# Block-selected attention with a gated MLP: who copies the selection rows, who normalises, and how the last outputs leave

## The chip, the cores and the metric

The kernel runs on one core of a Trainium2 chip. The metric is the device time of one execution in microseconds (us), the median of several runs. Engines are named as in the profile: PE is TensorE (matmuls; PEld are its weight loads), DVE is VectorE, ACT is ScalarE, POOL is GpSimd, and SP is the engine that issues the DMA transfers.

## What is computed

Attention over 4 batches of 8 heads, 768 positions, 64 values per head. For each query the keys are seen in 24 chunks of 32; an upper bound of the query's product with each chunk is made from the chunk's minimum and maximum, and only the 6 best chunks, causally masked, take part. The result is the input of a gated MLP block.

```python
# attention, per head; chunk = 32, top_k = 6
ub = sum(maximum(q * k_min, q * k_max))           # per query and chunk, causal
sel = the 6 chunks with the largest ub
attn = softmax(where(sel & causal, q @ k.T / 8, -1e9))
x = attn @ v                                      # heads side by side: (4, 768, 512)
# the MLP block
h = gelu_tanh(x @ w_in)                           # 512 -> 1024
u, v = h[..., :512], h[..., 512:]
v_n = (v - mean(v)) / sqrt(var(v) + 1e-6) * g_ln
v_s = w_sg @ v_n + b_sg[:, None]                  # over the positions, 768 x 768
out = x + (u * v_s) @ w_out
```

## The kernel before

The 32 heads are worked in 16 pairs (p = 0 to 15, two heads i = 0, 1 on 64 partitions each). Pairs 0 to 3 belong to batch 0 and so on; every four pairs, a batch of the MLP block (b = 0 to 3) follows, mixed with the scores of later pairs.

Each operation of the program is recorded once, by a call of `P.op` (or of the helper `flex`, L429 to L442), with an engine, a tag and what it reads and writes. The order of the work is not the order of the text: `TABLE` at the end holds, for each engine, the list of the operations' numbers in the order in which that engine runs them, the PSUM slot of each tile, the number of idle matmuls ahead of an operation (`filler`) and the engine of those operations that may run on several (`engine`). `place` and `link` turn this into one in-order queue for each engine and into semaphore waits. So an operation that waits holds everything behind it on its engine. SP's queue holds all transfers, loads, transposing transfers and stores alike. On POOL an operation marked `shift` also waits for its neighbour.

The tags that the text uses, with the pair or batch behind them:

- ktr, qtr (L524): K and Q of a pair transposed on PE, three 128-column matmuls each; kev, qev (L435, L438): the copies of these from PSUM to KA, qT; kmm (L563): minimum and maximum of each chunk on DVE, four instructions for a pair; wsub: their difference; rel (L435, L437): relu of qT; qcast, vcast, kcast (L435, L438): casts to bf16 into QA, vx, kbx.
- kT (L587), dt_x (L882): transposing transfers on SP, of K for pairs 12 to 15 and of the attention output (xT) for batches 1 and 2.
- ub (L662, L709): the bounds on PE; utr, m8, dn, dt (L718, L729, L734, L737): transposed on DVE, the sixth largest found by max8, compared, and transposed back into Dt. For the pairs from 4 on, `select_full` works two pairs at a time. qd (L742): the rows of Dt, 32 partitions by 576 for each head, are put into QA[w][i], where 32 spare rows carry the mask into the score matmul. Before, qd is a transfer on SP.
- sc (L778, L818): scores, in pieces of 1024 columns; exp (L784, L833): their exponential on ACT; aff (L789, L840): the causal mask of the diagonal blocks on POOL; pv, pvd (L856, L863): the product with V, pvd for the masked diagonal; rcp, xs (L871, L873): the division into XS.
- hv, gv, bns, bna (L905, L909, L914, L916): the v half, its gelu and statistics per 128 positions; var, rstd, nmr (L918, L920, L922): the reciprocal deviation, raised to the power on POOL; vhat (L928 on ACT, L933 on DVE): the normalised v, six tiles of 128 x 512 per batch.
- hu, gu (L945, L950): the u half; pt (L962): w_sg times vhat, which needs all six vhat of its batch; vs, gt (L968, L972): scale, bias and gate on DVE; ou (L981): the last product; os (L988): the residual sum into one of three buffers osb; st (L992): the store, 128 x 512 fp32.

PSUM is used in two halves: two slots of 1024 columns for scores, and four of 512 for the rest.

Of the kernel before, what the change touches and what calls it, by code (L numbers as in the profile page):

```python
# [261 lines left out]
def _build(nc, ctx, q, k, v, w_in, g_ln, w_sg, b_sg, w_out, out):
    B, H, S, DH = q.shape
    DM = H * DH
# [428 lines left out]
    def select_full(pairs, u, v_):  # L693
# [45 lines left out]
        for x, p in enumerate(pairs):  # L739
            for i in range(2):  # L740
                w, g0 = p % NW, 32 * (2 * (1 - i) + x)
                P.op("sp", lambda e, w=w, i=i, g0=g0: e.dma_start(  # L742
                    QA[w][i][g0:g0 + 32, LO:S], Dt[v_][g0:g0 + 32].rearrange("p a b -> p (a b)")), dmac(590),
                    ("qd", p, i), reads=[("Dt", v_)], writes=[("QD", w, i)], dma=f"qd{w}_{i}", xfer=150)
# [133 lines left out]
    def xtrans(b, dk):  # L878
        src = XS[:, b % 2, dk]
        rd = [("XS", b % 2, 2 * dk), ("XS", b % 2, 2 * dk + 1)]  # L880
        if (b, dk) in DXT:
            P.op("sp", lambda e: e.dma_start_transpose(xT[b % 2][:, dk, :].rearrange("p (t x) -> p t x", x=128),  # L882
# [13 lines left out]
    def moe_h(b):  # L896
# [28 lines left out]
        for qt in range(NT):  # L925
# [6 lines left out]
            else:  # L932
                o = P.op("dve", lambda d, qt=qt: d.tensor_scalar(vhat[s][:, qt, :], vg[qt], mv[s][:, qt, 0:1],  # L933
                                                                 rstd[s][:, qt:qt + 1], op0=ALU.subtract,
                                                                 op1=ALU.mult),
                         (456, 548), ("vhat", b, qt), port=True,
                         reads=[("vg", qt), ("mv", s, qt), ("nmr", s), ("rstd", s)], writes=[("vhat", s, qt)])
# [16 lines left out]
    def moe_g(b):  # L954
        s = b % 2
        for tg in range(2):
# [19 lines left out]
            for qt in range(3 * tg, 3 * tg + 3):  # L976
                t = ps_g.tile((2, 3) if b < B - 1 else None)

                def ou(e, t=t, qt=qt):
# [7 lines left out]
                os_ = (b * NT + qt) % 3  # L987
                P.op("dve", lambda d, t=t, qt=qt, os_=os_: d.tensor_tensor(  # L988
                    osb[os_][:].rearrange("p (a x) -> p a x", x=128),
                    t.ap()[:, 0:DM].rearrange("p (a x) -> p a x", x=128), XS[:, b % 2, :, qt, :], op=ALU.add), dve(DM), ("os", b, qt),  # L990
                    reads=[t] + [("XS", b % 2, hh) for hh in range(H)], writes=[("osb", os_)], ps=[t])
                P.op("sp", lambda e, qt=qt, os_=os_: e.dma_start(  # L992
                    bass.AP(out.tensor, (b * S + 128 * qt) * DM, [[DM, 128], [1, DM]]), osb[os_][:]), dmac(),
                    ("st", b, qt), reads=[("osb", os_)], dma=f"o{os_}", xfer=680)
# [208 lines left out]
```

## Time and profile before

| | us |
|---|---|
| median of 3 runs (lowest, highest) | 219.81 (219.38, 221.41) |
| the profiled execution | 220.97 |
| its span, first to last instruction | 219.1 |
| PE busy | 205.8 |
| DVE busy | 185.9 |
| ACT busy | 169.5 |
| POOL busy | 93.2 |

The mean granted clock of TensorE is 0.982 of full. How to read the rows: a row of a timeline has the start, the length (several instructions of one kind merged), the engine, the line, the operation, what it writes and reads, and in brackets the idle time before it and what ended it. A row of a group has the line, the count, the busy time and the mean of one in ns. A row of waits has who waited for whom: the sum in us, the number of times and the longest. A row of the chain has start, length, engine and line. "SPq" rows are issues of transfers. Ends of matmuls are modelled, so a PE that is busy is not always at its peak.

### The profile page before, as it was taken

The page shows a single profiled execution, that of the slowest core. Times are in us where ns is not written, and L with a number is a line of the kernel's source. Part 1 is how long each engine was busy: PE and PEld are TensorE (multiplying, and loading weights), DVE is VectorE, ACT ScalarE, POOL GpSimd, SP SyncE. Part 2 cuts the span into 40 slices and gives each one's busy share as a digit, 9 for nine tenths or more (in the row PEclk, how much of TensorE's full clock was granted, in tenths as well). Part 3 has the DMA queues.
Part 4 walks back from the last instruction along what each step waited for, and adds up shares of the span by engine and source line. Part 5 has one row for each costly group of instructions (what it writes and reads, how often), then busy time and mean ns, then how long its engine had stood idle before and what let it go on. Part 6 is the DMA issues. An engine that isn't in the chain of part 4 may idle for free.

```text
span 219.1 us, 5967 instructions
## 1 busy us (share of the span) xinstructions
PE 205.8 (94%) x2357; PEld 134.1 (61%) x2357; DVE 185.9 (85%) x536; ACT 169.5 (77%) x256; POOL 93.2 (43%) x130
## 2 busy tenths in 40 slices
PE   7799999999999999997998989998799999999991
PEld 3477777846767577783355666776545669545640
DVE  3889999799999999998799987985896876968982
ACT  3778999979899899998668888998768978575000
POOL 8434699894374556464023537185102414002000
PEclk9879999999999999998899999999999999999999
DMA  7999999993999988947999849642955004000325
GB/s 153 249 219 205 223 211 375 294 237 124 248 225 238 208 231 200 225 81 135 263 233 179 141 81 224 75 113 56 217 105 124 0 0 146 3 0 0 144 87 201
DMA packets 95067, 35.48 MB, mean 162 GB/s; under 512 B 89280, under 2 KB 90048, under 8 KB 95040
## 3 DMA queue, kind: packets, MB, share of 16 engines
q1 hardware_dynamic: 95040, 35.11, 72.6%
q8 instruction: 18, 0.29, 0.6%
q14 instruction: 9, 0.07, 0.1%
HBM read 24.77 MB, written 6.29 MB: 142 GB/s over the span
## 4 chain that ended last, share of the span: by engine, by line
PE 63%; DVE 16%; ACT 11%; DMA 4%; issue 3%; SPq 0%; DVEq 0%
PE PSG L962 11%; PE PSG L945 7%; PE PSG L905 7%; PE PSC L778 7%; PE PSG L524 6%; ACT E L784 5%; PE PSG L856 4%; PE PSG L981 4%; DMA QA<-Dt 4%; DVE osb L988 3%; PE PSG L709 3%; PE PSC L818 3%; PE PSG L662 3%; DVE Wall L563 2%; DVE U L718 2%
## 5 line engine op out<-in xcount | busy, mean ns | idle before, releaser
L784 ACT ACTIVATE E<-PSC 128x1024 bf16<-128x1024 f32 (+1 forms) x72 | 63.4, 916 | 8.2 <-PE PSC L778 7.0
L778 PE MATMUL PSC<-QA,KA 128*128 128x128 bf16 (+2 forms) x336 | 37.2, 246 | 2.2 <-ACT E L784 1.2
L962 PE MATMUL PSG<-wsgT,vhat 128*128 128x384 bf16 x192 | 35.3, 326 | 0.6 <-DVE vhat L933 0.6
L789 POOL TENSOR_SCALAR_AFFINE_SELECT E<-E 128x768 bf16<-128x768 bf16 x24 | 21.1, 885 | 30.6 <-ACT E L784 30.2
L778 PEld LDWEIGHTS PSC<-QA,KA 128*128 128x128 bf16 x336 | 24.3, 98 | 12.6 <-ACT E L784 3.2
L438 POOL CAST QA<-qT 64x768 bf16<-64x768 f32 (+1 forms) x24 | 20.6, 860 | 22.1 <-ACT qT L435 13.4
L905 PE MATMUL PSG<-winb,xT 128*128 128x512 bf16 x96 | 24.4, 397 | 1.8 <-DVE XS L873 1.1
L962 PEld LDWEIGHTS PSG<-wsgT,vhat 128*128 128x128 bf16 x192 | 17.8, 98 | 11.8 <-ACT qT L435 1.0
L563 DVE TENSOR_REDUCE Wall<-PSG 128x12 f32<-128x384 f32 x48 | 24.7, 540 | 0.3 <-PE PSG L524 0.2
L945 PE MATMUL PSG<-xT,winb 128*128 128x384 bf16 x128 | 24.4, 327 | 0.0
L950 ACT ACTIVATE uT<-PSG 128x384 bf16<-128x384 f32 x32 | 15.5, 490 | 11.3 <-PE PSG L945 10.6
L981 PE MATMUL PSG<-woutb,uT 128*128 128x512 bf16 x96 | 23.7, 379 | 0.0
L909 ACT ACTIVATE vgb<-PSG 128x512 f32<-128x512 f32 x24 | 14.3, 598 | 11.0 <-PE PSG L905 10.9
L968 DVE SCALAR_TENSOR_TENSOR PSG<-PSG,glnT,bsgbc 128x384 f32<-128x384 f32 x32 | 19.5, 618 | 2.4 <-PE PSG L962 2.3
L920 POOL TENSOR_TENSOR rstd<-rstd,neghalf 128x6 f32<-128x6 f32 x4 | 5.3, 1330 | 37.5 <-DVE rstd L918 37.5
L833 ACT ACTIVATE E<-PSC 128x1024 bf16<-128x1024 f32 (+1 forms) x24 | 20.7, 918 | 0.2
L856 PE MATMUL PSG<-vx,E 128*128 128x65 bf16 x480 | 19.9, 194 | 0.4 <-DVE osb L988 0.3
L988 DVE TENSOR_TENSOR osb<-PSG,XS 128x512 f32<-128x512 f32 x24 | 16.0, 683 | 5.0 <-PE PSG L981 4.0
L914 DVE BATCH_NORM_STATS2 stats<-vgb 128x6 f32<-128x512 f32 x24 | 16.2, 681 | 3.2 <-ACT vgb L909 3.0
L856 PEld LDWEIGHTS PSG<-vx,E 128*128 128x128 bf16 x480 | 17.3, 98 | 2.3 <-DVE osb L988 0.6
L873 DVE TENSOR_TENSOR XS<-PSG,rden 128x384 bf16<-128x384 f32 x32 | 17.6, 554 | 0.6
L972 DVE TENSOR_TENSOR uT<-PSG,uT 128x384 bf16<-128x384 f32 x32 | 17.3, 550 | 0.5
(106 smaller groups left out, 370.8 us busy)
## 6 DMA issues: line engine op xcount, KB each, us to landing
qn<-in_q_dram SPq DMA_DIRECT2D x32, 192.0 KB, 4.5
vn<-in_v_dram SPq DMA_DIRECT2D x16, 384.0 KB, 5.5
out_dram<-osb SPq DMA_DIRECT2D x24, 256.0 KB, 2.7
kn<-in_k_dram SPq DMA_DIRECT2D x24, 192.0 KB, 4.6
uT<-in_moe_w_sg_dram SPq DMA_DIRECT2D x4, 384.0 KB, 5.8
vgb<-in_moe_w_in_dram SPq DMA_DIRECT2D x3, 512.0 KB, 9.1
kn<-in_k_dram SPq DMA_DIRECT2D x4, 384.0 KB, 4.5
QA<-Dt SPq DMA_DIRECT2D x24, 36.0 KB, 2.6
```

The costliest lines, as they stand in the source:

```text
L438: return e.tensor_copy(dst(), src())
L563: P.op("dve", lambda d, m=m, op=op, t=t, hf=hf: d.tensor_reduce(W[w][:, m, 12 * hf:12 * hf + 12], t.ap()[:, 0:TG].rearrange("p (c x) -> p ...
L778: r = e.matmul(t.ap()[:, o:o + n], KA[w][i][:, 128 * kb:128 * kb + 128], QA[w][i][:, q0:q0 + n], start=True, stop=True)
L784: P.op("act", lambda e, t=t, c0=c0, c1=c1, i=i: e.activation(E[es][:, i, c0:c1], t.ap()[:, 0:c1 - c0], ACTF.Exp, scale=SCALE), act(c1 - c0 ...
L789: P.op("pool", lambda g, ev=ev: g.affine_select(ev, ev, pattern=[[0, NT], [1, 128]], compare_op=ALU.is_ge, fill=0.0, base=0, channel_multi ...
L833: P.op("act", lambda e, t=t, c0=c0, c1=c1, n=n: e.activation(E[es][:, :, c0:c1], t.ap().rearrange("p (i x) -> p i x", i=2)[:, :, 0:n], ACT ...
L856: r = e.matmul(t.ap()[:, 65 * qb:65 * qb + 65], E[es][:, i, a:a + 128], vx[w][:, kb, i, :], start=first, stop=False, skip_group_check=True)
L905: r = e.matmul(t.ap()[:, 0:F], xT[s][:, dk, 128 * qt:128 * qt + 128], winb[:, dk, F:DFF], start=(dk == 0), stop=(dk == NDK - 1))
L945: r = e.matmul(t.ap()[:, 0:TG], winb[:, dk, 128 * fb:128 * fb + 128], xT[s][:, dk, TG * tg:TG * tg + TG], start=(dk == 0), stop=(dk == NDK ...
L962: r = e.matmul(t.ap()[:, 0:TG], vhat[s][:, sb, 128 * fb:128 * fb + 128], wsgT[:, sb, TG * tg:TG * tg + TG], start=(sb == 0), stop=(sb == N ...
L981: r = e.matmul(t.ap()[:, 0:DM], gT[s][:, fb, 128 * qt:128 * qt + 128], woutb[:, fb, :], start=(fb == 0), stop=(fb == NF - 1))
L988: P.op("dve", lambda d, t=t, qt=qt, os_=os_: d.tensor_tensor(osb[os_][:].rearrange("p (a x) -> p a x", x=128), t.ap()[:, 0:DM].rearrange(" ...
```

## The change

Four things are edited in the program, and the whole table is written anew.

1. qd becomes a `flex` operation: a copy on POOL, or on DVE or ACT where the table says so. Of the 24, POOL has 14, ACT five (qd_4_1, qd_5_1, qd_9_1, qd_10_0, qd_11_0), DVE five (qd_10_1, qd_11_1, qd_13_0, qd_15_0, qd_15_1).
2. vhat may also run on POOL, as a tensor_scalar with two per-partition scalars. Of the 24, POOL has 14 (0_1, 0_2, 0_4, 0_5; 1_0, 1_1, 1_2, 1_3, 1_5; 2_3; 3_0, 3_2, 3_4, 3_5), ACT four (0_3, 1_4, 3_1, 3_3), DVE six (0_0 and five of batch 2). Before, DVE had 19 and ACT five.
3. For the last three position blocks of the last batch, os and st are made in halves of 256 columns, the sum goes into the buffers qn (free by then) in place of osb, and a store of the last batch may be issued by ACT; four are (st_3_2, st_3_4_0, st_3_5_0, st_3_3_256).
4. The engine of the transposing transfers becomes a name that the table may change. It does not: all stay on SP.

```diff
-                P.op("sp", lambda e, w=w, i=i, g0=g0: e.dma_start(
-                    QA[w][i][g0:g0 + 32, LO:S], Dt[v_][g0:g0 + 32].rearrange("p a b -> p (a b)")), dmac(590),
-                    ("qd", p, i), reads=[("Dt", v_)], writes=[("QD", w, i)], dma=f"qd{w}_{i}", xfer=150)
+                flex("pool", ("dve", "act"), lambda w=w, i=i, g0=g0: QA[w][i][g0:g0 + 32, LO:S],
+                     lambda g0=g0: Dt[v_][g0:g0 + 32].rearrange("p a b -> p (a b)"), NSEL, ("qd", p, i), [("Dt", v_)],
+                     [("QD", w, i)], shift=True)
...
-                o = P.op("dve", lambda d, qt=qt: d.tensor_scalar(vhat[s][:, qt, :], vg[qt], mv[s][:, qt, 0:1],
+                o = P.op(eng, lambda d, qt=qt: d.tensor_scalar(vhat[s][:, qt, :], vg[qt], mv[s][:, qt, 0:1],
...
+                last, os_ = b == B - 1 and qt > 2, (b * NT + qt) % 3
+                dst = qn[os_][:].rearrange("p i t d -> p (i t d)")[:, 0:DM] if last else osb[os_][:]
+                names = [("qn", os_, 0), ("qn", os_, 1)] if last else [("osb", os_)]
+                for c0, c1 in ((0, DM // 2), (DM // 2, DM)) if last else ((0, DM),):
+                    P.op("dve", lambda d, t=t, qt=qt, dst=dst, c0=c0, c1=c1: d.tensor_tensor(
...
+                    o = P.op(ENG.get("_".join(str(x) for x in tag), "sp"), lambda e, qt=qt, dst=dst, c0=c0, c1=c1: e.dma_start(
+                        bass.AP(out.tensor, (b * S + 128 * qt) * DM + c0, [[DM, 128], [1, c1 - c0]]), dst[:, c0:c1]), dmac(),
...
     "filler": (
-        "50:8 "),
+        "49:8 58:2 83:2 "),
```

Number 49 is ktr_0_0, 58 is qtr_0_0 and 83 is ktr_1_0. The new lists, given by tag where the text below speaks of them:

- PE, the start: ktr_0_0 ktr_0_1 qtr_0_0 qtr_0_1 ktr_1_0 ktr_1_1 ub_0 (before: ktr_0_1 ktr_0_0 qtr_0_1 qtr_0_0 ktr_1_1 ub_0 qtr_1_0 qtr_1_1 ktr_1_0). DVE: kmm_0 four times, qev_0_1, wsub_0, kmm_1 four times, then the selection of pair 0 (before: kev_0 twice, kmm_0 four times, rel_0, wsub_0, two of kmm_1, the selection, the other two of kmm_1). kev_0 and rel_0 are on ACT.
- PE, into batch 1: pvd_7_1 pv_7_0 pvd_7_0 ktr_11_1 sc_8_1_0 sc_8_1_1 qtr_12_0 sc_8_1_2 ktr_10_1 ktr_10_0 hv_1_1 sc_8_0_1 sc_9_1_1 hv_1_0 (before: pvd_7_1 ktr_11_1 sc_8_1_2 sc_8_1_0 ktr_10_0 sc_8_1_1 ktr_10_1 hv_1_1 hv_1_0 sc_8_0_0). POOL does qd_8_1 and qd_8_0 behind aff_7_0. kev_11_1 (two instructions) goes from ACT to DVE, qd_9_1 is on ACT.
- PE, the end of hv in batch 1: hu_1_2_0 hv_1_4 hu_1_3_1 ub_10 hu_1_3_0 hu_1_0_1 qtr_13_1 hu_1_0_0 qtr_13_0 hu_1_1_1 qtr_12_1 hu_1_2_1 hu_1_1_0 perm_12 pt_1_0_1. POOL: rstd_1 vhat_1_1 vhat_1_5 vhat_1_0 vhat_1_2 vhat_1_3 aff_8_1. perm_12 is a small permutation by matmul (L602).
- PE, around 131 us before: pt_1_0_3 sc_8_0_2 sc_9_0_1 ub_12 sc_10_1_2 (before: sc_9_0_1 pv_8_1 pvd_8_1 sc_10_1_0). rel_12 and rel_14 go from ACT to DVE.
- PE, in batch 3: the six hv, then hu hu ou_2_3 ou_2_4, six hu, ou_2_5, then pt. POOL: rstd_3 and the four vhat.
- DVE, the end: os_3_2 gt_3_1_2 os_3_1 os_3_0 os_3_4_256 os_3_4_0 os_3_5_0 os_3_5_256 os_3_3_256 os_3_3_0. The last number is the half's first column.

Other casts and evictions change engines too: nine casts and mask rows leave POOL for ACT and seven come back, and evictions are exchanged between DVE and ACT (on balance DVE takes two more of them and three more rel).

More of the change, by code (lines that the diff above doesn't have):

```diff
@@ L494, in _build @@
     QRUN = [0] * 16
+    TENG = "sp"
     KRUN = [0] * 16
@@ L586, in kside_full @@
                  ("kcast", p, i), [("kn", s, 0), ("kn", s, 1), ("kbi", n, i)], [("kbx", n, i)])
-            P.op("sp", lambda e, i=i: e.dma_start_transpose(
+            P.op(ENG.get(f"kT_{p}_{i}", TENG), lambda e, i=i: e.dma_start_transpose(
                 KA[w][i][:].rearrange("p (t x) -> p t x", x=128), kbx[n][:, i].rearrange("p t c -> p (t c)")), dmac(1250),
@@ L881, in xtrans @@
         if (b, dk) in DXT:
-            P.op("sp", lambda e: e.dma_start_transpose(xT[b % 2][:, dk, :].rearrange("p (t x) -> p t x", x=128),
+            P.op(ENG.get(f"dt_x_{b}_{dk}", TENG), lambda e: e.dma_start_transpose(xT[b % 2][:, dk, :].rearrange("p (t x) -> p t x", x=128),
                                                        src.rearrange("p t c -> p (t c)")), dmac(1250), ("dt_x", b, dk),
@@ L932, in moe_h @@
             else:
[L933 to L936, printed above, removed]
+                o = P.op(eng, lambda d, qt=qt: d.tensor_scalar(vhat[s][:, qt, :], vg[qt], mv[s][:, qt, 0:1],
+                                                               rstd[s][:, qt:qt + 1], op0=ALU.subtract,
+                                                               op1=ALU.mult),
+                         (456, 548) if eng == "dve" else (590, 640), ("vhat", b, qt), port=True,
                          reads=[("vg", qt), ("mv", s, qt), ("nmr", s), ("rstd", s)], writes=[("vhat", s, qt)])
-            o.alts = {"act": (704, 809), "dve": (456, 548)}
+            o.alts = {"act": (704, 809), "dve": (456, 548), "pool": (590, 640)}
         for fb in range(NF):
@@ L986, in moe_g @@
                      writes=[t], alloc=t)
[L987 to L994, printed above, removed]
+                last, os_ = b == B - 1 and qt > 2, (b * NT + qt) % 3
[3 more added lines that the diff above has]
+                    P.op("dve", lambda d, t=t, qt=qt, dst=dst, c0=c0, c1=c1: d.tensor_tensor(
+                        dst[:, c0:c1].rearrange("p (a x) -> p a x", x=128),
+                        t.ap()[:, c0:c1].rearrange("p (a x) -> p a x", x=128), XS[:, b % 2, c0 // 128:c1 // 128, qt, :],
+                        op=ALU.add), dve(c1 - c0), ("os", b, qt) + ((c0,) if last else ()),
+                        reads=[t] + [("XS", b % 2, hh) for hh in range(c0 // 64, c1 // 64)],
+                        writes=names if not last else [("qn", os_, c0 // 256)], ps=[t])
+                    tag = ("st", b, qt) + ((c0,) if last else ())
+                    o = P.op(ENG.get("_".join(str(x) for x in tag), "sp"), lambda e, qt=qt, dst=dst, c0=c0, c1=c1: e.dma_start(
+                        bass.AP(out.tensor, (b * S + 128 * qt) * DM + c0, [[DM, 128], [1, c1 - c0]]), dst[:, c0:c1]), dmac(),
+                        tag, reads=names if not last else [("qn", os_, c0 // 256)],
+                        dma=f"o{os_ + 3 * last}_{c0}", xfer=680 if not last else 360)
+                    if b == B - 1:
+                        o.alts = {"sp": (610, 610), "act": (571, 571)}
     SEL, GRP, UB, u = {}, {}, {}, 0
```

19 lines of the change are left out of this document (15 added, 4 removed), and 115 rows, old and new, of the table TABLE.

## The prediction

> **What bounds the kernel now.** I read the page's busy shares, then the table of stretches, then the waits, and last the timeline and the chain where TensorE's clock or busy time falls. In a stretch's row stand its length, the busy time of each engine and, behind the last bracket, TensorE's granted clock.
>
> ```profile
> PE 205.8 (94%) x2357; PEld 134.1 (61%) x2357; DVE 185.9 (85%) x536; ACT 169.5 (77%) x256; POOL 93.2 (43%) x130
> ```
>
> ```profile
> 44.00:98.00 54.00, 53.14 (x605) 37.62 (x603) 51.87 (x163) 49.47 (x83) 31.06 (x42) 1.00 0.92 203
> 98.00:106.00 8.00, 6.05 (x32) 2.58 (x30) 6.21 (x12) 6.50 (x10) 3.07 (x5) 0.79 0.89 163
> ...
> 170.00:211.00 41.00, 41.00 (x361) 25.43 (x361) 33.25 (x69) 23.97 (x33) 7.11 (x8) 1.00 0.11 39
> ```
>
> TensorE is full from 170 to 211 us and nearly so from 44 to 98. It does the same matmuls after the change, so what can move is the start, the hole at 98 to 106, a few gaps between 116 and 157 and the tail. What leaves VectorE elsewhere is worth nothing by itself.
>
> ```profile
> PEld PSC L778 <- ACT E L784: 3.2, 7, 0.8
> ...
> PE PSC L778 <- DMA QA<-Dt: 0.9, 2, 0.6
> ```
>
> TensorE waits 0.9 us in all for the transfers that the change removes; the exponentials on ScalarE (ACT) hold it longer.
>
> **The start.** Four idle matmuls are added, two ahead of qtr_0_0 and two ahead of ktr_1_0, and the first K evictions go from VectorE to ScalarE.
>
> ```profile
> 8.39 0.52 PE L524 MATMUL PSG<-identF,kn 128*128 128x128 f32 x3 [0.97 <-DMA kn<-in_k_dram]
> 9.52 0.93 PE L662 MATMUL PSG<-qT,Wall 64*32 64x288 f32 x8 [0.61 <-DVE Wall L573]
> ```
>
> ```profile
> 10.00:11.00 1.00, 1.00 (x12) 0.38 (x6) 0.87 (x2) 0.09 (x1) 0.00 (x0) 0.50 1.23 276
> ```
>
> ```profile
> 1.25 4.02 PE PSC L359 x9
> ...
> 7.15 1.85 DVE Wall L563 x4
> ...
> 9.52 2.12 PE PSG L662 x18
> 11.63 1.93 PE PSG L524 x9
> ...
> 15.61 1.22 PE PSG L662 x18
> ...
> 49.13 0.66 PE PSG L524 x6
> ...
> 55.75 0.65 PE PSG L945 x4
> ```
>
> After idle times of 0.97 and 0.61 us the clock is 0.50: the 18 matmuls of ub_0 take 2.12 instead of 1.22 us and the next nine 1.93 instead of 0.99, 1.84 lost. An idle matmul takes 4.02/9 = 0.45 us, so two of them cover 0.9 of the 0.97; I take the dip as avoided. But the new VectorE order has all four kmm_1 reductions ahead of the first selection instead of two: two more, at 1.85/4 each, give 0.95 back. Net -0.9, between -1.9 (nothing given back) and +0.5 (the dip stays and the idle matmuls delay qtr_0).
>
> The Trainium skill, "TensorE: Matmul & The Clock Gate", Part 1, says that the clock falls after at least one idle window of about 3.4 us. By that rule gaps of 0.97 and 0.61 us would not have dropped it and the added matmuls would be worth nothing; the row with 0.50 says otherwise, and I go by the row.
>
> **98 to 106 us.** The rows for the scores of pair 8 come late, and the second half clock follows.
>
> ```profile
> 99.45 0.61 PE L778 MATMUL PSC<-QA,KA 128*128 128x384 bf16 x4 [0.50 <-ACT E L784]
> 100.46 0.55 PE L524 MATMUL PSG<-identF,kn 128*128 128x128 f32 x3 [0.39 <-ACT KA L435]
> 101.65 3.30 PE L905 MATMUL PSG<-winb,xT 128*128 128x512 bf16 x8 [0.65 <-DMA xT<-XS]
> 105.28 0.65 PE L778 MATMUL PSC<-QA,KA 128*128 128x128 bf16 x7 [0.34 <-DMA QA<-Dt]
> ```
>
> ```profile
> 96.30 4.20 SPq L882 DMA_TRANSPOSE xT<-XS  x2
> ...
> 101.18 0.71 SPq L742 DMA_DIRECT2D QA<-Dt  x1
> ```
>
> ```profile
> 191.10 1.73 PE PSG L905 x8
> ```
>
> Waits of 0.50 + 0.39 + 0.65 + 0.34 = 1.88, and eight matmuls in 3.30 instead of 1.73: 3.45 in all. The copy of the rows stood on SP behind two transposing transfers, from 96.30 on. On POOL it needs no queue: the 0.34 goes, and two evictions (kev_11_1) leave ScalarE. The transposes stay on SP, and hv_1_1 still needs the last of them, so most of the 0.65 stays. Whether the clock dips again I can't tell: about 1.5 us of idle time caused it at the start, and about as much is left here. I take half of the 1.57: -1.5 in all, between 0 and -3.2.
>
> **Normalisation.** Fourteen vhat go to POOL; VectorE keeps 6 of 19, ScalarE 4 of 5. No row shows a tensor_scalar on POOL; the nearest are casts of the same size and, as an upper end, one that was held up.
>
> ```profile
> L438 POOL CAST woutb<-osb x1: 611/611/611, 66.9 to 66.9; 128x512 bf16<-128x512 f32 x1
> ```
>
> ```profile
> L438 POOL CAST vx<-vn x14: 826/832/1407, 21.2 to 172.5; 128x768 bf16<-128x768 f32 x14
> ```
>
> ```profile
> 109.59 1.04 PE L905 MATMUL PSG<-winb,xT 128*128 128x512 bf16 x4
> ...
> 112.79 1.33 POOL L920 TENSOR_TENSOR rstd<-rstd,neghalf 128x6 f32<-128x6 f32 x1 [11.65 <-DVE rstd L918]
> ...
> 117.84 1.14 PE L962 MATMUL PSG<-wsgT,vhat 128*128 128x384 bf16 x6 [0.60 <-DVE vhat L933]
> ```
>
> I take 0.61, between 0.61 and 1.41. In batch 1 the last group of hv ends at 109.59 + 1.04 = 110.6 and rstd at 112.79 + 1.33 = 114.1; vhat was there by 117.8. With 0.5 for nmr and five vhat on POOL it is 114.6 + 5 x 0.61 = 117.7, the same. TensorE meanwhile has seven hu groups of 0.65, ub_10 (1.2, as ub_0 at full clock), three transposes of 0.33 and the small perm_12, to 117.6: the wait of 0.60 shrinks, -0.2, between -0.6 and, at 1.41 each (121.7), +3.5. In batches 0 and 3 four vhat on POOL (2.4) stand behind the same 4.0 us from the last hv to nmr (114.6 - 110.6), 6.4 in all. To cover them TensorE has seven hu groups, five transposes and two score groups in batch 0, about 6.9, and eight hu and three ou (0.86, as a group of hv) in batch 3, 7.8: nothing; at 1.41 each, 3.2 more, +2.6 and +1.7. Batch 2 moves one.
>
> The Trainium skill, "GPSIMD Engine Reference", 3.1, has 1.8 cycles per element at 1.2 GHz, 768 ns for 512 elements; by that estimate batch 1 would be 0.8 later than I take it and the sum would be 0.8 higher.
>
> **Selection rows.** Of 24 copies (32 partitions by 576 elements), POOL gets 14, ScalarE 5, VectorE 5; SP's queue loses all 24.
>
> ```profile
> L438 POOL COPY KA<-INDF 64x768 bf16<-64x768 bf16 x8 | 6.6, 823 | 0.3
> ...
> L435 ACT ACTIVATE rT<-qT 128x576 f32<-128x576 f32 x11 | 7.5, 683 | 0.1
> ...
> L438 DVE COPY xT<-PSG 128x768 bf16<-128x768 bf16 x5 | 2.8, 553 | 0.6 <-PE PSG L890 0.6
> ```
>
> By these rows 0.62 on POOL (823 x 576/768), 0.68 on ScalarE, 0.41 on VectorE, whose 13 vhat fewer pay for it. They count at the gaps where rows or exponentials were awaited:
>
> ```profile
> 130.71 0.60 PE L778 MATMUL PSC<-QA,KA 128*128 128x128 bf16 x7 [0.70 <-ACT E L784]
> ...
> 149.16 0.60 PE L778 MATMUL PSC<-QA,KA 128*128 128x128 bf16 x7 [0.59 <-DMA QA<-Dt]
> ...
> 156.11 1.02 PE L905 MATMUL PSG<-winb,xT 128*128 128x512 bf16 x4 [1.10 <-DVE XS L873]
> ```
>
> At 149 us the transfer goes: -0.55 (0 to -0.6; next late is the exponential two score tiles back). At 131 rel_12 (0.68) leaves ScalarE and ub_12 stands ahead of the scores: -0.5 (0 to -0.7). At 156 TensorE waits for xT, a transpose that stays on SP with less ahead of it: -0.2 (-0.7 to +0.6).
>
> Against that: POOL's order gets 14 x 0.62 + 14 x 0.61 = 17 us of work, less about 2 for casts that leave it; its masks (aff), which gate pvd, stand behind. Its busy share rises from 43 to about 50%, so it is a matter of single late masks: +0.8 (0 to +2). ScalarE gets eight instructions before 62 us (qcast_4_1, mrow_1_1_0, two row copies, vhat_0_3, three wev) and loses, the exchanged evictions set against each other, three; five more at 0.5 to 0.8, in a stretch where TensorE seldom waits for it: +0.6 (0 to +2).
>
> **The tail.**
>
> ```profile
> 213.69 1.03 PE L981 MATMUL PSG<-woutb,uT 128*128 128x512 bf16 x4
> ```
>
> ```profile
> 213.27 0.69 DVE L988 TENSOR_TENSOR osb<-PSG,XS 128x512 f32<-128x512 f32 x1 [0.41 <-DMA out_dram<-osb]
> 214.46 1.29 DVE L988 TENSOR_TENSOR osb<-PSG,XS 128x512 f32<-128x512 f32 x2 [0.50 <-DMA out_dram<-osb]
> ```
>
> ```profile
> DMA to landing us min/median/max: 2.0/2.1/2.9
> ```
>
> The last three outputs wait 0.41 + 0.50 for their buffer; in qn they don't. The last matmul ends at 213.69 + 1.03 = 214.7; two halves of about 0.40 (estimated, a little over half of 0.69) follow, so VectorE ends at 215.5 instead of 215.75, and the last store is 128 KB on one of two queues (2.0 to 2.9 us, the lower end likelier): -0.6, between -0.2 and -1.1.
>
> **Sum.** -0.9 - 1.5 - 0.2 - 0.55 - 0.5 - 0.2 - 0.6 = -4.45; +0.8 + 0.6 = +1.4; net -3.05. The profiled execution took 220.97 us, 1.87 more than its span of 219.1; it would take 217.9. It stands 1.16 above the median of the three runs, 219.81, which becomes 216.8.
>
> **The rivals.** (a) POOL becomes the bound, slower. If a vhat costs 1.41 there, as the held-up cast did, pt_1 comes 3.5, pt_0 2.6 and pt_3 1.7 us later, in place of the -0.2: 216.8 + 8.0 = 224.8; it decides from about 1.05 us each, where the three delays sum to 3. For it: the row with 1407 against a median of 832, and a vhat of VectorE that ended with a POOL cast beside it after 1049 ns against a median of 541. Against it: those medians. The Trainium skill, "SBUF — State Buffer", section on the two separate sides, says that VectorE and GpSimd share a port pair under an exclusive lock, the loser blocked for the whole instruction; the two maxima agree.
>
> ```profile
> L933 DVE TENSOR_SCALAR vhat<-vgb,mv,rstd x19: 505/541/1049, 57.4 to 200.1; 128x512 bf16<-128x512 f32 x19
> ```
>
> (b) The transfers were hidden anyway and the waits change hands: both clock dips stay (+0.9 and +0.8 against my sum, and the gaps at 131 and 156 stay for ScalarE's and the transposes' sake, +0.7): 216.8 + 2.4 = 219.2. For it: 0.9 us in the row of waits, against 3.2 for the exponentials. (c) Both dips go, nothing is given back and no mask is late: -0.95 - 0.8 - 1.4 more: 213.6.
>
> **How the numbers follow.** Forecast 0.45, (a) 0.17, (b) 0.26, (c) 0.12. A difference of under 1% (2.2 us) is about what can't be told from none; the forecast's own spread (215.0 to 218.3) puts a seventh of it there. Faster: 0.38 + 0.12 + 0.06 of (b) = 0.56; the same: 0.07 + 0.18 + 0.02 of (a) = 0.27; slower: 0.15 + 0.02 = 0.17. The range from (c) to the mild end of (a), 213.4 to 220.6, leaves out some 0.2.
>
> **What would show it.** Clock 1.00 from 9 to 16 us and ub_0 in about 1.2 us show the start right. No wait of TensorE on Dt's rows, and the first hv of batch 1 in 0.43 or 0.22 per matmul, show the hole. POOL's vhat at 0.6 to 0.8 us shows the normalisation; 1 us and more, with pt waiting on POOL, makes me wrong towards (a). No idle time of VectorE behind out_dram, and an end about 3.8 us behind the last matmul instead of 4.4, show the tail. New waits of pvd on POOL's masks or of scores on ScalarE beyond 1.4 us make me wrong towards (b).

## The result, and the profile after

The changed kernel takes 242.65 us (median of 4 runs, 242.51 to 244.37) against 220.36 us (219.38 to 221.41): 1.103 times the time before, with a 95% interval of 1.095 to 1.111. The forecast was 216.8 us, with a range of 213.4 to 220.6. It is wrong in sign. A median here is over all executions of a kernel, while a ratio leaves out those in which the chip was in a slower state, so the two can differ by some tenths of a per cent. Rival (a), POOL as the bound, is what happened, at a price well above the one that the rival was given.

The profiled execution of the change has a span of 242.5 us (before 219.1). The page's busy shares come first, then the waits of TensorE and the price of a vhat (median in the middle of the three figures, in ns).

```profile
PE 209.4 (86%) x2346; PEld 135.8 (56%) x2361; DVE 185.5 (77%) x536; ACT 171.4 (71%) x257; POOL 128.3 (53%) x156
```

```profile
PE PSG L963 <- POOL vhat L934: 18.0, 3, 7.3
```

```profile
L934 POOL TENSOR_SCALAR vhat<-vgb,mv,rstd x14: 2070/2073/2347, 58.2 to 221.0; 128x512 bf16<-128x512 f32 x14
```

VectorE's and ScalarE's busy times hardly change. POOL has 35 us more. TensorE waits three times, 18.0 us in all, for vhat on POOL; a vhat there takes 2.07 us, not 0.61.

To see whether anything else was lost, cut each execution at two events of each batch: the end of nmr, from which vhat can start, and the start of the first vs, which needs pt and so all six vhat. In the kernel before, VectorE's rows are these:

```profile
57.24 0.15 DVE L922 SCALAR_TENSOR_TENSOR nmr<-mv,rstd 128x6 f32<-128x6 f32 x1
61.57 0.62 DVE L968 SCALAR_TENSOR_TENSOR PSG<-PSG,glnT,bsgbc 128x384 f32<-128x384 f32 x1
...
114.36 0.12 DVE L922 SCALAR_TENSOR_TENSOR nmr<-mv,rstd 128x6 f32<-128x6 f32 x1
119.21 0.60 DVE L968 SCALAR_TENSOR_TENSOR PSG<-PSG,glnT,bsgbc 128x384 f32<-128x384 f32 x1
...
166.04 0.17 DVE L922 SCALAR_TENSOR_TENSOR nmr<-mv,rstd 128x6 f32<-128x6 f32 x1 [1.44 <-POOL rstd L920]
170.06 0.63 DVE L968 SCALAR_TENSOR_TENSOR PSG<-PSG,glnT,bsgbc 128x384 f32<-128x384 f32 x1 [0.19 <-PE PSG L962]
...
198.51 0.17 DVE L922 SCALAR_TENSOR_TENSOR nmr<-mv,rstd 128x6 f32<-128x6 f32 x1 [0.41 <-POOL rstd L920]
202.06 0.62 DVE L968 SCALAR_TENSOR_TENSOR PSG<-PSG,glnT,bsgbc 128x384 f32<-128x384 f32 x1 [0.23 <-PE PSG L962]
```

After the change, VectorE's rows and between them POOL's:

```profile
57.95 0.17 DVE L923 SCALAR_TENSOR_TENSOR nmr<-mv,rstd 128x6 f32<-128x6 f32 x1
58.22 8.52 POOL L934 TENSOR_SCALAR vhat<-vgb,mv,rstd 128x512 bf16<-128x512 f32 x4 [0.30 <-DVE nmr L923]
69.00 0.63 DVE L969 SCALAR_TENSOR_TENSOR PSG<-PSG,glnT,bsgbc 128x384 f32<-128x384 f32 x1 [6.73 <-PE PSG L963]
...
121.71 0.17 DVE L923 SCALAR_TENSOR_TENSOR nmr<-mv,rstd 128x6 f32<-128x6 f32 x1
121.98 10.30 POOL L934 TENSOR_SCALAR vhat<-vgb,mv,rstd 128x512 bf16<-128x512 f32 x5 [0.30 <-DVE nmr L923]
134.54 0.63 DVE L969 SCALAR_TENSOR_TENSOR PSG<-PSG,glnT,bsgbc 128x384 f32<-128x384 f32 x1 [8.14 <-PE PSG L963]
...
181.73 0.17 DVE L923 SCALAR_TENSOR_TENSOR nmr<-mv,rstd 128x6 f32<-128x6 f32 x1 [1.46 <-POOL rstd L921]
186.39 0.63 DVE L969 SCALAR_TENSOR_TENSOR PSG<-PSG,glnT,bsgbc 128x384 f32<-128x384 f32 x1 [0.62 <-PE PSG L963]
...
214.52 0.17 DVE L923 SCALAR_TENSOR_TENSOR nmr<-mv,rstd 128x6 f32<-128x6 f32 x1 [0.27 <-POOL rstd L921]
214.79 8.25 POOL L934 TENSOR_SCALAR vhat<-vgb,mv,rstd 128x512 bf16<-128x512 f32 x4 [0.30 <-DVE nmr L923]
225.30 0.63 DVE L969 SCALAR_TENSOR_TENSOR PSG<-PSG,glnT,bsgbc 128x384 f32<-128x384 f32 x1 [6.57 <-PE PSG L963]
```

The stages, as differences of these rows (end of nmr is start plus length; the last stage ends with the span):

| stage | before, us | after, us | difference |
|---|---|---|---|
| start to nmr of batch 0 | 57.4 | 58.1 | +0.7 |
| nmr to first vs, batch 0 | 4.2 | 10.9 | +6.7 |
| first vs of batch 0 to nmr of batch 1 | 52.9 | 52.9 | 0.0 |
| nmr to first vs, batch 1 | 4.7 | 12.7 | +7.9 |
| to nmr of batch 2 | 47.0 | 47.4 | +0.4 |
| nmr to first vs, batch 2 | 3.9 | 4.5 | +0.6 |
| to nmr of batch 3 | 28.6 | 28.3 | -0.3 |
| nmr to first vs, batch 3 | 3.4 | 10.6 | +7.2 |
| to the end | 17.0 | 17.2 | +0.2 |

The four normalisations lose 22.5 of the 23.4 us. The five other stages together lose 0.9 where the forecast had them gain about 2.85. The execution before holds the two half-clock stretches that the prediction read at 10 and 102 us, so an execution of the old kernel without them would make these five look slightly worse.

Behind each long wait TensorE's clock falls as well. In the rows of stretches the granted clock stands behind the last bracket:

```profile
66.00:71.00 5.00, 4.12 (x14) 2.21 (x15) 1.26 (x3) 0.00 (x0) 3.54 (x5) 0.50 0.91 197
...
132.00:136.00 4.00, 3.57 (x13) 2.07 (x14) 1.31 (x4) 0.49 (x1) 2.67 (x4) 0.50 0.22 52
...
223.00:227.00 4.00, 3.82 (x13) 1.83 (x14) 1.18 (x2) 0.00 (x0) 0.04 (x1) 0.50 0.00 0
```

The first pt tile therefore takes 2.08 us where it took 1.14, which adds about 0.9 to each of the three stages.

```profile
132.43 2.08 PE L963 MATMUL PSG<-wsgT,vhat 128*128 128x384 bf16 x6 [7.29 <-POOL vhat L934]
```

The waits before these stretches were 5.5, 7.3 and 5.2 us. The granted clock falls 3.5, 4.5 and 3.8 us into them, stays at half for 6.8 us, and is back at 1.00 only 4.8, 4.1 and 5.5 us after TensorE has gone on. The Trainium skill, "TensorE: Matmul & The Clock Gate", Part 1, has the clock fall after an idle window of about 3.4 us; in these three waits the trace agrees with it.

### The profile page after: what moved, and what is told of

It reads as the page before. It is cut to its first block, busy times and chain, and to the rows that moved or that the text cites. A ratio compares the mean times of both kernels' runs of the same rounds, so it can differ in the third digit from the quotient of the medians.

```text
span 242.5 us, 5963 instructions
## 1 busy us (share of the span) xinstructions
PE 209.4 (86%) x2346; PEld 135.8 (56%) x2361; DVE 185.5 (77%) x536; ACT 171.4 (71%) x257; POOL 128.3 (53%) x156
## 4 chain that ended last, share of the span: by engine, by line
PE 53%; DVE 15%; POOL 14%; ACT 6%; DMA 6%; issue 3%; POOLq 1%; SPq 1%; DVEq 0%
PE PSG L963 15%; POOL vhat L934 10%; PE PSC L779 7%; PE PSG L906 5%; PE PSG L982 5%; PE PSG L857 4%; PE PSG L525 4%; DMA vn<-in_v_dram 3%; DMA kn<-in_k_dram 3%; PE PSG L946 3%; DVE stats L915 2%; ACT E L785 2%; PE PSG L864 2%; DVE Wall L564 2%; POOL rstd L921 2%
## 5 line engine op out<-in xcount | busy, mean ns | idle before, releaser
L963 PE MATMUL PSG<-wsgT,vhat 128*128 128x384 bf16 x192 | 41.1, 367 | 18.0 <-POOL vhat L934 18.0
L963 PEld LDWEIGHTS PSG<-wsgT,vhat 128*128 128x128 bf16 x192 | 19.9, 108 | 33.1 <-issue 25.0
L934 POOL TENSOR_SCALAR vhat<-vgb,mv,rstd 128x512 bf16<-128x512 f32 x14 | 29.4, 2112 | 1.2 <-DVE nmr L923 1.2
L906 PE MATMUL PSG<-winb,xT 128*128 128x512 bf16 x91 | 21.8, 379 | 4.1 <-DVE XS L874 1.6
L946 PE MATMUL PSG<-xT,winb 128*128 128x384 bf16 x128 | 23.7, 327 | 0.0
L982 PE MATMUL PSG<-woutb,uT 128*128 128x512 bf16 x86 | 21.3, 379 | 0.5
L435 ACT ACTIVATE qT<-PSG 128x384 f32<-128x384 f32 x24 | 11.5, 490 | 13.6 <-PE PSG L525 13.4
L438 POOL CAST QA<-qT 64x768 bf16<-64x768 f32 (+1 forms) x20 | 16.3, 821 | 8.7 <-ACT qT L435 6.3
L992 DVE TENSOR_TENSOR osb<-PSG,XS 128x512 f32<-128x512 f32 x21 | 14.3, 687 | 6.1 <-PE PSG L982 5.8
```

Of the source, the lines that this page charges most:

```text
L906: r = e.matmul(t.ap()[:, 0:F], xT[s][:, dk, 128 * qt:128 * qt + 128], winb[:, dk, F:DFF], start=(dk == 0), stop=(dk == NDK - 1))
L934: o = P.op(eng, lambda d, qt=qt: d.tensor_scalar(vhat[s][:, qt, :], vg[qt], mv[s][:, qt, 0:1], rstd[s][:, qt:qt + 1], op0=ALU.subtract, op ...
L946: r = e.matmul(t.ap()[:, 0:TG], winb[:, dk, 128 * fb:128 * fb + 128], xT[s][:, dk, TG * tg:TG * tg + TG], start=(dk == 0), stop=(dk == NDK ...
L963: r = e.matmul(t.ap()[:, 0:TG], vhat[s][:, sb, 128 * fb:128 * fb + 128], wsgT[:, sb, TG * tg:TG * tg + TG], start=(sb == 0), stop=(sb == N ...
L982: r = e.matmul(t.ap()[:, 0:DM], gT[s][:, fb, 128 * qt:128 * qt + 128], woutb[:, fb, :], start=(fb == 0), stop=(fb == NF - 1))
```

## The experiments

Twelve kernels were run, each beside runs of the kernel before on the same chip.

**The change with the vhat given back.** The 14 go from POOL's list to VectorE's, right behind nmr of their batch (in batches 0 and 2 behind VectorE's own vhat).

```diff
-vhat_0_1:pool vhat_0_2:pool vhat_0_4:pool
+vhat_0_1:dve vhat_0_2:dve vhat_0_4:dve
...
-vhat_3_2:pool vhat_3_0:pool vhat_3_4:pool vhat_3_5:pool
+vhat_3_2:dve vhat_3_0:dve vhat_3_4:dve vhat_3_5:dve
```

> The changed kernel with one part undone: the 14 vhat that POOL had are VectorE's again, behind nmr of their batch; lists, row copies, tail and start as changed. Theory A (the price of a vhat on POOL, 2.1 us instead of the 0.61 taken, on the way to pt in batches 0, 1 and 3, and the clock dips behind those waits): PE's wait for POOL vhat (18.0 us) goes and the time falls from 242.7 to 216 to 220; the rest of the change is worth about what the other terms say, -2.85 against 220.4. Theory B (the new lists themselves, POOL's queue with row copies and late masks, or the load order, cost the time): 230 us and more; PE waits on aff, qd or loads in place of vhat.

225.09 us, ratio 1.018 (1.014 to 1.022). 1.8% are 4.0 us above the kernel before, where the change is 22.3 us above it: POOL's vhat are worth about 18 us. Theory A holds for these, but its second half missed: the rest of the change doesn't gain, it costs some 4 us in this form. By the same stages of its profiled execution, it gains 1.7, 1.0, 0.3 and 1.8 us in the stages between and at the end, and loses 0.2 at the start and 4.4, 2.0, 0.5 and 1.0 between nmr and vs. So what is lost here is lost between nmr and vs, where VectorE's list was laid out for vhat elsewhere; that the layout is the cause is argued, not shown. Part of the 4.4 is a half clock from 63.2 to 66.6 us: with the old start (below) the same lists wait as long but without it, and lose 3.0 there. Five vhat take 4.01 us there, and a weight transpose ahead of pt waits behind two evictions and a reduction on VectorE:

```profile
57.62 4.01 DVE L934 TENSOR_SCALAR vhat<-vgb,mv,rstd 128x512 bf16<-128x512 f32 x5
...
63.28 0.90 PE L476 MATMUL PSG<-identF,uT 128*128 128x128 f32 x3 [2.77 <-DVE Wall L564]
```

**The vhat alone.** The kernel before, with the same 14 on POOL behind rstd.

```diff
-                o = P.op("dve", lambda d, qt=qt: d.tensor_scalar(vhat[s][:, qt, :], vg[qt], mv[s][:, qt, 0:1],
+                o = P.op(eng, lambda d, qt=qt: d.tensor_scalar(vhat[s][:, qt, :], vg[qt], mv[s][:, qt, 0:1],
```

> The kernel before with one part of the change: the same 14 vhat are on POOL, behind rstd of their batch; everything else as before. Theory A: each takes about 2.1 us; with VectorE's 19 partly free nothing is gained; 4, 5 and 4 in a row make 8.4, 10.5 and 8.4 us in batches 0, 1 and 3, of which PE waits for some 15 to 18 us, and with a half-clock stretch behind each the time is 236 to 244. Theory B: a vhat takes under 1 us here, as it waits less for the port, and the time is 220 to 226.

246.58 us, ratio 1.117 (1.112 to 1.122): theory A, 2.6 us above its upper end. This one part, put into the old lists, makes the kernel 26 us slower.

**The price by itself.** Elementwise instructions alone, three or more of each kind in a row. ts2 is vhat's form, with two per-partition scalars; new gives each instruction an output of its own.

```diff
+            for _ in range(3):
+                ts2(g, new("y", Y), x, 512)
+            for _ in range(3):
+                g.tensor_scalar(new("y", Y), x[:, 0:512], 0.25, 0.25, op0=ALU.subtract, op1=ALU.mult)
+            for _ in range(3):
+                g.tensor_scalar(new("y", Y), x[:, 0:512], 0.25, None, op0=ALU.mult)
...
+            for _ in range(3):
+                g.tensor_copy(new("y", Y), x[:, 0:512])
```

> The computation is left out: only elementwise instructions are run, to price them. On POOL, three each, VectorE idle: tensor_scalar as in vhat (128x512, fp32 to bf16, two per-partition scalars), with two immediates, with one immediate, with one scalar, a cast of the same size, vhat's form with fp32 output, with bf16 input, of 256 and of 1024 columns; then vhat's form and casts beside VectorE at work, and VectorE's and ScalarE's own price of a vhat. Theory A1 (the instruction is slow on POOL by itself): 2.0 to 2.1 us with VectorE idle, growing with the columns (about 1.0 for 256, 4.1 for 1024), the cast about 0.61. Theory A2 (it is slow for the port that it shares with VectorE): 0.6 to 0.8 us alone, 2 us only beside VectorE. Whether the per-partition scalars, the second operation or the type make it slow: the form whose time falls to the cast's 0.61 tells.

POOL's timeline, VectorE idle (start, length of three, in us): vhat's form; two immediates; one immediate; one scalar; the cast; vhat's form with fp32 output; with bf16 input.

```profile
6.76 6.19 POOL L40 TENSOR_SCALAR Y<-x,sc 128x512 bf16<-128x512 f32 x3 [6.33 <-DVE D L40]
12.92 5.70 POOL L79 TENSOR_SCALAR Y<-x 128x512 bf16<-128x512 f32 x3
18.58 4.40 POOL L81 TENSOR_SCALAR Y<-x 128x512 bf16<-128x512 f32 x3
22.97 4.64 POOL L83 TENSOR_SCALAR Y<-x,sc 128x512 bf16<-128x512 f32 x3
27.57 1.73 POOL L85 CAST Y<-x 128x512 bf16<-128x512 f32 x3
29.28 6.19 POOL L40 TENSOR_SCALAR z<-x,sc 128x512 f32<-128x512 f32 x3
35.45 6.18 POOL L40 TENSOR_SCALAR Y<-xb,sc 128x512 bf16<-128x512 bf16 x3
```

A1 holds: 6.19/3 = 2.06 us with VectorE idle, as in the kernel. The type makes no difference and per-partition scalars little (1.55 against 1.47 with one operation); arithmetic does. One operation costs 1.47 us, two 1.90 to 2.06, the cast of the same tile 0.6. Groups of 256 and 1024 columns:

```profile
L40 POOL TENSOR_SCALAR Y<-x,sc 128x1024 bf16<-128x1024 f32 x2 | 7.5, 3780 | 0.0
L40 POOL TENSOR_SCALAR Y<-x,sc 128x256 bf16<-128x256 f32 x3 | 3.6, 1218 | 0.0
```

(3780 - 1218)/768 = 3.34 ns for a column, and 0.36 us fixed. The 768 ns for 512 elements that the prediction cites from the Trainium skill, "GPSIMD Engine Reference", 3.1, stand there as the best case, for a tight loop; this instruction takes 2.7 times as long. Section 7 of the same page, on pitfalls, has 4 cycles per element for a chain of dependent fp32 operations; at the 1.2 GHz of 3.1 that is 3.33 ns, an estimate that the measured slope matches. That the instruction runs such a chain no run shows.

Beside each other the two engines slow down. VectorE's vhat by itself and beside POOL's, then POOL's:

```profile
L40 DVE TENSOR_SCALAR D<-dx,sc 128x512 bf16<-128x512 f32 x2 | 1.0, 539 | 0.0
...
L40 DVE TENSOR_SCALAR D<-dx,sc 128x512 bf16<-128x512 f32 x12 | 8.8, 803 | 0.0
L40 POOL TENSOR_SCALAR Y<-x,sc 128x512 bf16<-128x512 f32 x4 | 8.7, 2191 | 0.0
```

VectorE goes from 0.54 to 0.80, POOL from 2.07 to 2.19. So VectorE at work adds 6% to POOL's price and doesn't make it: A2 falls.

**One vhat in each batch.** The kernel before, with 0_1, 1_1 and 3_2 on POOL.

> The kernel before with one vhat of batches 0, 1 and 3 on POOL (0_1, 1_1, 3_2), right behind rstd; the others as before. Alone, one vhat of 2.1 to 2.3 us on POOL stands beside 2.0 to 2.8 us of VectorE's own. Theory A (it is the row of four and five that costs): 220 to 221, the stage from nmr to the first vs in batch 0 4.2 us as before. Theory A2 (POOL's long instruction also slows VectorE's vhat beside it, 0.80 instead of 0.54 as in the price run): five at 0.8 are 4.0 instead of 2.8, +1.0 to +1.3 in batch 0, less in 1 and 3: 221.5 to 223.

219.47 us beside 219.51 us, ratio 0.999 (0.995 to 1.003): no change in time, as A has it. But batch 0 takes 4.8 us from nmr to the first vs where A has 4.2, so what A2 says is there too, at about half its size. A POOL vhat of 2.3 us lies beside five of VectorE, which takes 3.43 us for them:

```profile
57.11 3.43 DVE L933 TENSOR_SCALAR vhat<-vgb,mv,rstd 128x512 bf16<-128x512 f32 x5
...
57.18 2.35 POOL L933 TENSOR_SCALAR vhat<-vgb,mv,rstd 128x512 bf16<-128x512 f32 x1 [0.59 <-DVE nmr L922]
```

Nothing is won by the one that VectorE gives up: five slowed vhat (3.43) take longer than six undisturbed ones (2.83 us in a row further down).

**The row copies alone.** The kernel before with qd on engines, each behind its Dt.

```diff
-                P.op("sp", lambda e, w=w, i=i, g0=g0: e.dma_start(
-                    QA[w][i][g0:g0 + 32, LO:S], Dt[v_][g0:g0 + 32].rearrange("p a b -> p (a b)")), dmac(590),
+                flex("pool", ("dve", "act"), lambda w=w, i=i, g0=g0: QA[w][i][g0:g0 + 32, LO:S],
```

> The kernel before with one part of the change: the 24 row copies are made by engines (14 POOL, 5 ScalarE, 5 VectorE, as in the change), each put where its Dt is done in the order before; SP's queue loses them. The prediction's terms that belong to the copies alone: about -0.3 at the hole, -0.55 at 149 us, and against them up to +0.8 for POOL's masks and part of the +0.6 for ScalarE: 219.3 to 220.8 against 220.4, no PE wait on Dt's transfers. Rival: the copies cost more than they bring (the 4.6 us that the change without POOL's vhat is slower come from them): 222 to 225.

225.63 us, ratio 1.025 (1.021 to 1.030): the rival. The stages put it in one place: nmr of batch 0 comes at 59.0 instead of 57.4, and the first vs 7.4 us behind it instead of 4.2. Two of ScalarE's copies stand ahead of a gelu that the statistics need, and V's load comes earlier on the emptier queue, so that POOL's casts run beside VectorE's six vhat. The next run puts back these two copies and the two that POOL makes at the same place:

**The row copies without those of pairs 4 and 5.**

```diff
+                if p < 6:
+                    P.op("sp", lambda e, w=w, i=i, g0=g0: e.dma_start(
...
+                else:
+                    flex("pool", ("dve", "act"), lambda w=w, i=i, g0=g0: QA[w][i][g0:g0 + 32, LO:S],
```

> As the run with the row copies alone (225.6), but the four copies of pairs 4 and 5 stay transfers on SP, at their old places; the other 20 are engine copies as there. Theory A (5.1 of the 5.4 us were lost at 57 to 64 us: two copies on ScalarE ahead of a gelu that the statistics wait for, two on POOL, and V's load coming earlier, so that POOL's casts ran beside VectorE's six vhat, 5.11 us instead of 2.82): nmr_0 is back at 57.0, the first vs 4.2 us behind it, and the time 219 to 221, with about -2 at the hole and up to +1.8 at 92 us, where a mask row stands behind four copies on POOL. Rival (copies on engines lose wherever they stand): 223 to 225.5.

221.42 us, ratio 1.005 (1.001 to 1.009): slightly above A's range and far from the rival's. Batch 0 is back to 56.6 and 4.2, so these four copies are what cost it; how much is due to ScalarE's two and how much to the casts beside VectorE's vhat was not tested apart. ScalarE's two copies and VectorE's six vhat, first with all copies on engines:

```profile
52.69 1.37 ACT L435 ACTIVATE QA<-Dt 32x576 bf16<-32x576 bf16 x2
...
59.02 5.11 DVE L933 TENSOR_SCALAR vhat<-vgb,mv,rstd 128x512 bf16<-128x512 f32 x6
```

and with the four put back:

```profile
56.59 2.83 DVE L938 TENSOR_SCALAR vhat<-vgb,mv,rstd 128x512 bf16<-128x512 f32 x6
...
86.09 0.43 PE L783 MATMUL PSC<-QA,KA 128*128 128x256 bf16 x3 [1.70 <-POOL KA L438]
```

The last row is a loss that stays: a mask row behind four copies on POOL, which the scores of pair 6 wait for. The remaining 20 copies don't gain: the wait for Dt in the hole is gone, and 1.7 us here and 1.4 us at 128 us, where TensorE waits for VectorE's uT, are lost for it.

**The load order alone,** and **the start alone.** First the kernel before with the first 40 loads in the changed order (an excerpt of SP's list, by tag); then with all lists of the change up to the first hv.

```diff
-kn_2_0 kn_2_1 qn_2_0 qn_2_1 kn_3_0 kn_3_1 qn_3_1 qn_3_0 vn_0 kn_4_1 kn_4_0 vn_1
+kn_2_0 kn_2_1 kn_3_1 qn_3_0 qn_2_1 qn_2_0 kn_3_0 qn_3_1 qn_4_1 kn_4_0 kn_4_1 qn_4_0 vn_0 wi_0 vn_2 vn_1
```

> The kernel before with the first 40 loads on SP in the order of the change (K and Q of pairs 3 and 4 ahead of the first V, V of pairs 0 to 2 and w_in's first part later); nothing else. If the 4.6 us come from the loads (V awaited by POOL's casts at 24 and 30 us, w_in at 44): 221.5 to 223.5, PE waiting for vx and winb as in the change. If not: 220 to 221.

> The kernel before, with all lists of the change up to the first hv (the first 44 us: loads, idle matmuls, first evictions on ScalarE, reductions ahead of the first selection), and its own lists from there. The prediction's term for the start is -0.9 (+0.5 to -1.9): 219.5. Theory C1 (the 4.6 us arise in the first 44 us): 222 to 225. Theory C2 (they arise behind, where VectorE's list was laid out without the vhat): 219.5 to 220.9.

222.62 us, ratio 1.012 (1.006 to 1.017), and 222.63 us, ratio 1.011 (1.005 to 1.018). In the first, TensorE waits for the Q of pair 2, now behind two loads of pair 3:

```profile
16.73 0.52 PE L524 MATMUL PSG<-identF,qn 128*128 128x128 f32 x3 [1.36 <-DMA qn<-in_q_dram]
```

In the second the largest wait is at the joint of the two sets of lists, and it says little of the change itself:

```profile
45.70 1.88 PE L905 MATMUL PSG<-winb,xT 128*128 128x512 bf16 x4 [3.20 <-DVE KA L438]
```

**The start undone.** The first experiment's kernel with the old lists up to the first hv.

> The change with VectorE's 14 vhat (as in the first run, 225.1 us), and the lists of the kernel before up to the first hv. C1 (the first 44 us): 220 to 222. C2 (VectorE overfull behind 57 and 114 us, ub, Bn and row copies waiting behind vhat): 224 to 226.

224.91 us, ratio 1.020 (1.013 to 1.027), as with the new start (1.018). So the new start neither brings nor costs anything that this kernel shows; the 2.5 us of the two runs above don't add to the rest. C2's range holds.

**Room behind nmr.** The first experiment's kernel with two evictions and a vhat moved to ScalarE and perm_12 behind the first pt.

```diff
+kev_6_0_0:act kev_6_0_1:act vhat_0_5:act
-hu_1_1_0 perm_12 pt_1_0_1
+hu_1_1_0 pt_1_0_1 perm_12
```

> The change with VectorE's vhat (225.1), and room made behind nmr: kev_6_0 (two evictions) and vhat_0_5 go from VectorE to ScalarE, idle there for 3.2 us, and PE's perm_12 stands behind the first pt of batch 1. Theory (the 4.6 us that this kernel loses arise between nmr and the first vs, 8.56 and 6.75 us in batches 0 and 1 where the kernel before has 4.18 and 4.72, for lists laid out for vhat elsewhere): 221 to 223, these stages 6 to 7 and 4.5 to 5.5. Rival (the loss is in the other stages, or moves on behind them): 224.5 to 225.5.

224.37 us, ratio 1.018 (1.012 to 1.025): a miss. The stages become 7.55 and 6.74 us, where 6 to 7 and 4.5 to 5.5 were expected; the transpose ahead of pt now waits for the evictions on ScalarE:

```profile
61.80 0.90 PE L476 MATMUL PSG<-identF,uT 128*128 128x128 f32 x3 [2.24 <-ACT KA L435]
```

In batch 1 the first pt is done by 121 us, but vs comes at 123.8: VectorE has other reductions (Bn, L581) and max8 ahead of it. That the loss lies between nmr and vs stands; that these four moves lift it does not. What laying out these lists anew would give stays open.

**The tail alone.** The kernel before with the halves.

> The kernel before with the last part of the change alone: os and st of the last three position blocks in halves into qn, four of the last batch's stores issued by ScalarE. The prediction's term is -0.6 us (-0.2 to -1.1): 219.3 to 220.2 against 220.4, VectorE with no wait for out_dram. The rival, that the last store's landing sets the end anyway and halves gain nothing: 220.4 and above.

219.17 us beside 220.43 us, ratio 0.994 (0.991 to 0.996). About twice the forecast gain. Six halves take 2.48 us, 0.41 each (forecast 0.40), and none waits for out_dram:

```profile
211.66 2.48 DVE L991 TENSOR_TENSOR qn<-PSG,XS 128x256 f32<-128x256 f32 x6 [0.17 <-PE PSG L981]
```

**The hole and the tail.** That kernel with two row copies on POOL, qd_8_1 and qd_8_0 behind aff_7_1.

> The kernel before with the halved tail (219.2 alone) and two row copies, qd_8_1 and qd_8_0, on POOL behind aff_7_1; the other 22 stay transfers, all lists else as before. The prediction's term for the hole at 98 to 106 us, -1.5 (0 to -3.2): 217.7 (216 to 219.2). Rival (the transposes that xT waits for set the end of the hole anyway): 219 to 219.5.

217.98 us beside 219.51 us, ratio 0.991 (0.987 to 0.995): faster than the kernel before. Against the tail alone (0.991 to 0.996) the intervals overlap, so that the two copies gain anything in time is not shown; in the profiled executions the stage from the first vs of batch 0 to nmr of batch 1 is 0.7 shorter. TensorE with the tail alone:

```profile
104.13 0.60 PE L778 MATMUL PSC<-QA,KA 128*128 128x128 bf16 x7 [1.37 <-DMA QA<-Dt]
```

and with the two copies, where no such wait is left:

```profile
102.69 0.61 PE L783 MATMUL PSC<-QA,KA 128*128 128x128 bf16 x7
103.49 2.76 PE L910 MATMUL PSG<-winb,xT 128*128 128x512 bf16 x12 [0.20 <-ACT vgb L914]
```

## Why the prediction was wrong, step by step

**Normalisation: the step that failed.** "I take 0.61, between 0.61 and 1.41" was the price of a vhat on POOL; it takes 2.07 to 2.35 us, and the term of -0.2 came out at +22.5. The upper end was a held-up cast, and a cast does no arithmetic. The one row of arithmetic on POOL in the trace before was quoted in that very step, the pow of 128x6 in 1.33 us: six columns cost more there than a cast of 512. It didn't give the price of a subtract and multiply, but it showed that casts were no bound for it. The prediction's own formula was sound: with 2.1 us in place of 1.41 its delays of 3.5, 2.6 and 1.7 become 7.0, 5.4 and 4.5 (five, four and four vhat, 0.7 more each), against measured waits of TensorE of 7.3, 5.5 and 5.2 us in batches 1, 0 and 3. The half clock behind each wait adds about 0.9 to the stage; in batch 3 the remaining 1.1 of its 7.2 is work of TensorE that the new list has ahead of pt, not behind it. Rival (a)'s point of decision, 1.05 us, was passed twice over. Rival (b)'s mechanism, transfers that were hidden and waits that change hands, is what the row copies show; its time and (c)'s were nowhere near.

**The second dip.** The prediction counted the dips at the start and in the hole as losses to be won back, but had no term for a dip behind a new wait. Three came, of 6.8 us each.

**The start, -0.9.** Its mechanism was right: the clock stays at 1.00, and ub_0 takes 1.3 us.

```profile
10.00:11.00 1.00, 1.00 (x19) 0.41 (x11) 1.00 (x4) 1.00 (x2) 0.00 (x0) 1.00 1.23 274
```

Its value was not: nmr of batch 0 comes 0.7 later. TensorE waits 1.1 us at 13.5 us and 1.6 us at 44.7 us, for ScalarE and VectorE; with the tail alone it is 0.6 and 0.7 at these places. The changed load order stood in no term, and alone it costs 2.5 us. The dip was also a property of the one execution that was read: with the same PE list up to there and gaps of 0.77 to 1.00 us, the kernel with the tail alone shows 1.00.

```profile
10.00:16.00 6.00, 5.43 (x74) 3.73 (x70) 5.89 (x23) 4.51 (x10) 2.12 (x3) 1.00 1.32 231
```

Nor was it worth 1.84 us: the profiled executions of four kernels with the same lists up to there (vhat alone, tail alone, one vhat, hole and tail) have no dip, and nmr of batch 0 ends at 56.7 to 57.1 us in them, 0.3 to 0.7 earlier than in the one that was read. The times say as much: among 15 executions of the kernel before, the six with a mean clock of 0.998 or more have a median of 220.2 us, and the six below 0.993 one of 220.8, though each group spreads over more than a microsecond.

**The hole, -1.5.** The stage changes by 0.0 in the change, and by -0.7 where two copies alone are moved. The dip was the execution's here too: the tail alone and one vhat have none, and their stage is 52.2 us instead of 52.9, so it was worth 0.7 and not 1.57. The wait for Dt is 1.37 where there is no dip. In the change both are gone, but TensorE waits elsewhere in the stage, the longest time for the differences (wsub) that ub_10 needs:

```profile
118.63 0.72 PE L710 MATMUL PSG<-qT,Wall 64*32 64x288 f32 x16 [1.07 <-DVE Wall L574]
```

**Row copies, -0.55, -0.5 and -0.2.** The prices were right to 0.1 us: forecast 0.62 on POOL, 0.68 on ScalarE and 0.41 on VectorE, measured medians (rows below, in ns):

```profile
L438 POOL COPY QA<-Dt x14: 652/660/947, 54.0 to 178.7; 32x576 bf16<-32x576 bf16 x14
L435 ACT ACTIVATE QA<-Dt x5: 666/679/682, 55.2 to 154.3; 32x576 bf16<-32x576 bf16 x5
L438 DVE COPY QA<-Dt x5: 300/314/868, 145.8 to 189.6; 32x576 bf16<-32x576 bf16 x5
```

TensorE no longer waits for transfers of Dt, yet the stage from 119 to 166 us gains nothing (+0.4). Of its three gaps, the 0.70 for the exponential goes, the 0.59 for the transfer becomes 1.03 for a row copy that VectorE makes behind other work, and the 1.10 for XS becomes 1.65.

```profile
147.23 0.43 PE L779 MATMUL PSC<-QA,KA 128*128 128x256 bf16 x3 [1.03 <-DVE QA L438]
```

In the run of the copies alone, POOL's mask rows, ScalarE's gelu and VectorE's vhat beside POOL's earlier casts came late and cost 5.5 us, against the terms +0.8 and +0.6. The run with 20 copies alone puts these at +0.5% all told.

**The tail, -0.6.** Right in kind and too small: 1.4 us by itself (0.8 to 1.9, from the interval of the ratio). In the change VectorE doesn't wait for out_dram either, and the end comes 3.5 us behind the last matmul instead of 4.4; the stage still shows +0.2, since the half clock behind the last wait falls into it.

**The rule that was weighed and the rival's rule.** On the price of a vhat, the rows of casts and the best case cited beside them both lay far below. The Trainium skill, "SBUF — State Buffer", section on the two separate sides, has the loser of the port pair blocked for the whole instruction. In the price run VectorE's vhat took 0.80 us beside POOL instructions of 2.19, so it is not held for the whole of one. Nor does the vhat of 1049 ns that the prediction took for agreement show it: it began 0.78 us before the cast beside it ended, and held until then it would have taken 0.78 + 0.54 = 1.32 us.

## What to carry to other kernels

A bound must come from a row of the same kind: a cast, however much delayed, bounds no arithmetic, and where an engine has no such row the range has to reach far beyond it. A clock dip in one profiled execution is first compared with other executions before it is counted as time to be won. A transfer that is taken off a queue also lets the loads behind it start earlier, and the work that they trigger may fall beside an instruction that can't afford it, as V's cast did in batch 0.

## What was unexpected of the hardware

- A two-operation tensor_scalar on POOL costs 0.36 us and 3.34 ns a column (128 partitions), 2.06 us for 512; with one operation 1.47; a cast of the same tile 0.61; bf16 input makes it no faster.
- VectorE's tensor_scalar of 0.54 us takes 0.80 beside POOL's, and six beside its casts took 5.11 us instead of 2.83; POOL's takes 2.14 to 2.35 instead of 2.07.
- After waits of 5.2 to 7.3 us TensorE ran at half clock for another 4.1 to 5.5 us. Shorter waits are a matter of the execution: the same wait of 2.77 us was followed by 3.4 us of half clock in the run with the vhat given back and by none in the run with the start undone, and gaps of about one microsecond at the start had a dip behind them in some executions and not in others.
